# Whole-tensor loads in place of half loads in an attention and feed-forward kernel that plays a planned table

## The chip, the cores and the metric

The kernel runs on one core of a Trainium2 chip. The metric is the device time of one execution in microseconds (us). Everything below names the engines as the profile does: PE is TensorE's matmuls (PEld its weight loads), DVE is VectorE, ACT is ScalarE, POOL is GpSimd, SP is SyncE. SP computes nothing; it issues DMAs. An engine takes its instructions in the order in which they were put on its queue, and an instruction that waits holds up everything behind it on the same queue.

## The reference

Two stages follow each other. The first is a linear attention with a Hedgehog feature map over 8 batches, 8 heads, 576 positions and head size 64; the second is a feed-forward layer with a squared ReLU over the 4608 tokens.

```python
def phi(x):
    proj = np.einsum('bhsd,df->bhsf', x, w_phi)
    proj = proj - np.max(np.abs(proj), axis=-1, keepdims=True)
    return np.concatenate([np.exp(proj), np.exp(-proj)], axis=-1)
q_p, k_p = (phi(q), phi(k))
kv = np.einsum('bhsf,bhsd->bhfd', k_p, v)
z = np.sum(k_p, axis=2)
num = np.einsum('bhsf,bhfd->bhsd', q_p, kv)
den = np.einsum('bhsf,bhf->bhs', q_p, z)[..., None] + 1e-06
x = (num / den), tokens by 512
h = np.maximum(x @ w_in, 0.0)       # 512 x 2048
out = h * h @ w_out                 # 2048 x 512
```

## The kernel before

**Data.** All matmuls are in bfloat16. The loads convert from float32 on the way: GpSimd issues them (`load_x`, L341 to L354), and each q, k or v of a batch lands in a tile of 128 partitions (576 KB). Such a tile has four head pairs; batches 0 and 1 and the weights are loaded by a list of their own (`FIRSTS`, L359), and from batch 2 on `loads` (L378) issues two loads for each tensor, head pairs 0 to 1 and head pairs 2 to 3 (288 KB each). There are two buffers each for q, k and v.

**Attention of one batch.** k and q have to be transposed, so that head size lies on partitions. For batches 0 and 1 PE does it (L430) and DVE or ACT copies the result out. From batch 2 on, SP issues transposing DMAs (L419), five for k and five for q, each as soon as the part of the load that it reads has landed. kT has one buffer, qT has two. PE multiplies k with w_phi (L484), DVE takes the largest magnitude (L495) and subtracts it (L505), ACT takes the exponentials (L513; L529 in batches 0 and 1). POOL copies v into a tile with a column of ones (L466, L467) or, for the first parts of batches 0 and 1, scales v by an exponential of the maximum (L546). PE then forms kv, with the denominator as one more column (L579), in two halves of the heads, four products each; ACT or DVE copies it out (L594, L598). For each pair of 64-token groups PE projects q in two layouts (L625, L657), ACT takes the exponentials (L632), DVE and POOL prepare a scale (L664, L678, L687, L694), PE multiplies with kv (L725), and DVE finishes the quotient into a tile xo (L735, L742, L746). xo has three buffers. It is transposed into xT, by PE for batches 0 and 1 (L756, copied out at L761) and after that by a DMA that SP issues (L765).

**Feed-forward.** Nine chunks of 512 tokens. PE multiplies with w_in (L787), ACT takes the ReLU into hr (L792, three buffers), POOL squares it into h (L795, 30 buffers; DVE at L798 for chunks 7 and 8), PE multiplies with w_out (L818), DVE copies out (L835) and SP stores (L840, two DMAs for 128 tokens). The products of a chunk are mixed with the attention of later batches, so PE always has some of both to do. PSUM has eight banks, shared by all; the attention may hold seven.

**What sets the order.** The program is written as operations with engines, costs and dependences (`Plan.op`). A planner that is not part of the file has turned them into a table of numbers, `ORDER` (L93), one number for each operation in the order of their creation; a negative number stands for so many filling matmuls on PE (L384, warm-ups). `play` (L74) goes through the table, takes a buffer from a ring for an operation that is the first to use it, and emits the instructions. The waits that run on the chip are those that the data and the buffers need. The dependences and costs given to `op` served the planner alone: `load` (L293) makes each load depend on the issue of the one ahead, on a bound of 4096 descriptor rows, and, once 15 loads are queued, on the landing (`dma`, an operation without instructions) of the load two ahead. So in the order as planned two loads are outstanding.

Of the kernel before, what the change touches and what calls it, by code (L numbers as in the profile page):

```python
# [44 lines left out]
class Plan:  # L45
# [48 lines left out]
    7 9 11 6 13 15 17 19 10 1 2 8 4 5 -15 33 34 -3 50 54 51 16 -3 37 38 55 56 35 -1 72 39 52 36 57 59 53 73 74  # L94
    75 41 42 76 81 79 61 65 62 -6 94 40 -4 83 95 77 78 70 66 68 84 87 67 64 63 89 85 -2 43 44 18 -2 45 47 46 48
    -4 116 96 12 21 23 25 14 60 49 86 92 88 90 20 111 118 117 80 82 69 71 -1 100 102 58 91 115 114 97 93 27 29
    22 137 139 98 99 101 104 103 138 107 105 158 160 108 106 132 109 112 119 113 120 121 110 125 126 122 127
    159 133 136 135 134 140 128 153 154 161 157 179 123 129 124 141 142 146 147 130 131 155 156 181 143 144 148
    149 180 150 145 24 26 1465 1461 31 387 174 178 200 177 176 182 175 167 162 168 163 1462 169 164 1468 201
    170 165 171 202 1463 389 1466 1469 1470 1464 1467 166 183 214 215 151 216 188 184 189 152 195 198 199 197  # L100
    196 227 228 203 229 231 1471 185 190 218 186 1477 219 187 204 191 217 192 205 1472 1473 226 232 233 1478
    1474 1475 1476 1479 209 210 172 238 193 173 230 194 242 243 236 237 211 206 207 212 208 213 1480 239 244
    1481 247 1482 245 249 260 253 250 1494 1495 1490 256 257 246 240 1483 1486 241 234 1491 262 261 255 1487
    252 251 28 265 1508 30 220 222 267 221 223 224 225 266 235 1492 248 1489 1493 388 399 390 407 401 405 264
    258 254 259 1509 263 270 287 269 268 288 289 272 271 273 275 274 1510 1484 1496 391 393 1485 392 276 279
    278 303 306 305 277 308 309 310 304 280 281 290 307 32 1497 1501 1502 329 324 331 311 282 285 330 286 284
    283 1516 312 1504 1517 326 328 1505 327 325 332 394 1518 1506 1488 395 397 396 398 313 314 296 317 291 1507
    297 292 293 315 318 1511 316 298 299 300 294 400 1515 319 345 420 346 295 320 321 350 351 1519 301 347 322
    348 302 323 1498 1512 1522 349 1499 1513 1523 421 422 1520 1521 403 352 423 1526 1500 1514 402 371 373 372
    425 366 368 1527 353 1533 1525 354 1549 367 1534 369 1524 565 1535 567 1528 566 569 359 1532 333 427 426  # L110
    355 360 338 1529 1550 429 370 1530 424 428 1551 568 404 406 339 356 340 361 334 335 1539 362 341 363 357
    336 358 435 430 337 1536 374 1537 419 364 1546 365 342 437 436 1540 343 1541 344 438 439 571 1538 570 1531
    573 572 1555 1562 431 432 433 434 1547 1569 415 409 411 412 417 418 410 416 413 414 408 440 462 479 442 441
    443 1576 1577 1556 375 574 577 1548 589 579 583 1557 1573 464 376 380 1559 377 381 463 378 379 382 481 1558
    1542 480 483 482 1574 1560 1563 1564 444 484 383 384 486 485 575 0 1575 465 1561 487 446 447 453 445 506
    448 452 449 450 507 508 457 454 451 501 466 461 460 456 459 1552 1543 488 489 455 494 495 490 1553 458 1544
    576 591 593 509 1554 1579 504 1580 496 472 491 1566 385 492 497 473 498 493 467 474 468 475 476 1570 469
    470 471 503 502 745 1565 1581 747 1567 510 505 1571 386 1603 746 516 511 517 512 748 1503 499 477 580 603
    578 598 605 1585 513 518 514 519 515 520 521 604 1545 1589 1593 1597 1607 597 1572 1568 749 751 523 528 607
    526 524 1611 1615 600 599 601 527 529 530 1598 1616 581 582 478 500 522 1622 1623 1612 550 608 551 552 750  # L120
    752 602 525 1613 606 531 1624 753 1614 1600 1582 1630 609 610 1608 1601 1631 1583 553 755 1584 1632 585 586
    618 620 619 584 613 545 546 547 532 548 611 754 1609 612 1636 549 1637 1602 1610 1638 923 756 1640 1586
    1594 1595 554 1621 1587 1641 1642 1618 533 560 538 1625 590 592 587 1617 595 771 757 588 594 596 614 615
    1619 617 622 1596 925 1620 1588 621 534 539 555 684 1629 556 561 557 540 535 562 685 686 558 541 536 559
    542 1644 1633 563 564 537 1634 1604 1645 616 635 1605 924 662 663 664 636 639 637 638 758 630 631 632 624
    629 634 633 625 657 661 640 642 623 626 660 659 927 641 643 665 658 644 627 628 778 780 779 926 1639 1590
    650 1643 645 1591 666 687 929 928 1606 931 1592 646 651 679 728 730 1648 680 652 647 672 1647 653 729 731
    673 648 649 654 1651 769 1599 543 763 1578 761 775 759 667 674 1652 544 782 688 683 681 682 689 1626 1649
    1627 668 690 694 695 675 676 1675 696 691 669 670 692 671 693 697 698 1628 930 760 762 1679 706 701 783 708
    707 785 784 767 655 1683 705 703 704 702 781 1650 1646 1657 1661 1665 1687 709 710 786 723 726 724 764 788  # L130
    793 1688 1653 765 677 678 656 699 700 1669 794 1670 1676 1708 1694 727 787 1677 725 732 1695 1678 933 1712
    1662 1693 1697 770 776 772 773 774 1709 1710 1713 1663 777 795 789 790 791 792 766 768 820 815 798 822 1701
    821 738 739 800 799 1690 819 818 816 817 932 1103 1671 935 1635 1664 1696 1714 1691 1672 1720 1721 955 934
    953 797 1673 802 716 1666 717 740 741 711 733 718 712 734 1705 713 1706 719 714 735 1684 1658 801 736 742
    737 939 715 720 936 940 1674 1722 1692 1685 796 823 1659 1667 1668 1105 1660 1104 743 949 947 945 721 722
    951 937 1707 943 1689 812 806 842 843 844 804 805 803 808 807 809 810 811 813 837 838 814 840 841 839 956
    966 958 1654 1106 824 3 1655 1656 957 959 845 1107 1686 1109 1702 1680 1711 1715 830 1703 1681 846 968 831
    1719 825 826 832 847 852 848 853 833 967 1698 1704 1682 1699 1700 827 1723 849 854 1716 1717 1718 850 851
    828 855 856 834 1724 1729 970 1108 1733 859 860 908 829 938 1110 864 865 910 866 909 867 1111 1765 1769
    1773 863 862 861 868 969 881 886 887 961 884 885 744 835 857 941 836 858 1737 1741 963 888 1788 869 1744  # L140
    1742 874 1726 882 960 883 1745 1727 1113 889 1728 1738 962 964 875 870 876 1762 1739 1740 1763 911 1764
    1777 877 948 944 946 950 952 954 1020 976 1725 942 878 1021 978 1780 871 872 1022 873 1112 1789 890 1781
    965 1790 1746 1281 1730 1752 1747 1770 1753 1731 1114 1283 1782 1732 1778 977 980 971 903 906 907 972 973
    904 1771 912 1023 1754 1772 896 897 1784 1774 1751 1756 1775 905 974 1757 1758 918 891 892 1766 913 914 919
    1755 898 915 1785 1786 979 975 1767 1119 1117 1115 920 893 921 899 900 916 922 894 917 895 1743 879 1133
    1779 1127 1734 1759 1760 1116 1735 982 993 995 994 998 1000 999 1768 1001 984 981 983 996 1135 1736 1776
    997 1024 985 1002 986 988 990 1086 1087 1015 987 1016 1017 1018 989 1136 880 1783 1787 1791 991 992 1019
    1003 1025 1008 1748 1138 1137 1139 1749 1140 1026 1009 1030 1027 1801 1004 1031 1010 1032 1005 1006 1011
    1033 1028 1012 1007 1118 1795 1792 1793 1282 901 1131 1129 1120 1750 1805 1796 1034 1029 1088 1146 1147
    1042 1141 1142 1143 1044 1148 1013 1035 1121 1125 1123 1761 1809 1819 1823 1794 1827 902 1014 1036 1820  # L150
    1816 1810 1145 1821 1144 1043 1045 1817 1818 1811 1812 1822 1089 1284 1813 1814 1122 1150 1151 1064 1066
    1152 1059 1060 1061 1831 1832 1065 1153 1833 1842 1838 1824 1802 1062 1149 1063 1839 1843 1046 1825 1067
    1840 1285 1844 1826 1286 1124 1081 1085 1156 1037 1083 1038 1039 1041 1084 1068 1803 1040 1090 1157 1158
    1837 1841 1845 1860 1856 1861 1082 1857 1159 1804 1862 1287 1288 1047 1069 1070 1048 1834 1052 1071 1074
# [32 lines left out]
def kernel(  # L187
# [16 lines left out]
    NPR = H // 2  # L204
# [79 lines left out]
    queue, issues = [], []  # L284
# [77 lines left out]
    for n, what in enumerate(FIRSTS.split()):  # L362
        what, a = what.split(":")
        a, z = (int(x) for x in a.split("-"))
# [13 lines left out]
    def loads(b, dep):  # L378
        for name in "kvq":
            for a in range(0, NPR, 2):  # L380
                load_x(b, name, 32 * b - 120, dep, a, a + 2)
# [548 lines left out]
```

## Time and profile before

| | |
|---|---|
| median of 13 runs | 351.71 us |
| lowest, highest | 350.04, 357.43 us |
| the profiled execution's own time | 351.67 us |
| its span, first to last instruction | 349.9 us |
| granted TensorE clock | 1.00 |
| HBM read, written | 36.77 MB, 9.44 MB |
| loads of k, q, v in halves, issue to landing (median) | 5.4, 5.5, 6.0 us |
| transposing DMAs kT, qT, xT, issue to landing (median) | 5.3, 4.8, 3.1 us |

The profile is one execution taken by the hardware profiler. Its page gives busy time, 40 equal slices of 8.75 us with the busy share in tenths, the chain of work that ended last, groups of instructions and DMA issues. A row of a timeline has the start, the length, the engine, line, operation, tiles and shape, and in brackets the idle time just before it with what ended it. "SPq" is SP's queue; a wait of SPq is time in which nothing behind it on that queue could be issued.

### The profile page before, as it was taken

Reading aid. Unit: us, or ns where it says so; the run is one execution under the profiler, and the core shown is the slowest. Engines: PE = TensorE matmul, PEld = TensorE weight load, DVE = VectorE, ACT = ScalarE, POOL = GpSimd, SP = SyncE. Lnnn points to the kernel's source line nnn. Section 1 sums busy time; section 2 is a strip of 40 time slices with the busy share of each in tenths; the row PEclk is TensorE's granted clock in tenths of the full one; section 3 lists DMA queues with packets and bytes.
Section 4 is the critical chain, followed back from the end, with each engine's and each line's share of the span. In section 5 each row is a group of like instructions: output and inputs, shape, how many; then the busy total and the mean of one; then the engine's idle time right before and its main releaser. Section 6 shows DMA issues by size and latency. Waiting matters only on the chain.

```text
span 349.9 us, 10160 instructions
## 1 busy us (share of the span) xinstructions
PE 338.1 (97%) x4045; PEld 197.2 (56%) x4045; DVE 243.7 (70%) x553; ACT 242.2 (69%) x496; POOL 197.9 (57%) x305
## 2 busy tenths in 40 slices
PE   6899999989999999999999999998999999999995
PEld 4679777758645654565446544654546544544444
DVE  2999878985987898677766897767468446633531
ACT  4999997889488958895778649956795256703510
POOL 8957966848969672989397629945962020000000
PEclk9999999999999999999999999999999999999999
DMA  8999995998997993949986255784312323021134
GB/s 126 210 210 209 206 134 97 121 178 88 171 138 126 159 202 67 143 57 176 187 114 123 32 86 95 114 149 83 71 36 47 77 48 76 3 45 43 39 86 104
DMA packets 66527, 39.13 MB, mean 112 GB/s; under 512 B 46256, under 2 KB 60976, under 8 KB 66480
## 3 DMA queue, kind: packets, MB, share of 16 engines
q0 software_dynamic: 16144, 18.35, 36.4%
q1 hardware_dynamic: 50176, 20.00, 33.7%
q8 instruction: 31, 0.51, 0.6%
q10 hardware_dynamic: 160, 0.13, 0.2%
q14 instruction: 16, 0.13, 0.1%
HBM read 36.77 MB, written 9.44 MB: 132 GB/s over the span
## 4 chain that ended last, share of the span: by engine, by line
PE 78%; DMA 8%; DVE 5%; ACT 4%; SPq 3%; issue 1%; POOL 0%; DVEq 0%; POOLq 0%
PE one L787 31%; PE one L818 30%; PE one L725 5%; PE one L579 5%; DMA kT<-xk 2%; SPq L419 2%; PE one L625 2%; PE one L657 2%; DMA qT<-xq 2%; PE one L484 2%; DMA xk<-in_k_dram 2%; DVE mk L495 1%; DMA xT<-xo 1%; ACT hr L792 1%; ACT kph L513 1%
## 5 line engine op out<-in xcount | busy, mean ns | idle before, releaser
L795 POOL TENSOR_TENSOR h<-hr 128x512 bf16<-128x512 bf16 x112 | 114.4, 1039 | 52.8 <-ACT hr L792 49.1
L787 PE MATMUL one<-xT,win 128*128 128x512 bf16 (+2 forms) x768 | 138.5, 326 | 2.0 <-DVE xo L746 1.0
L818 PE MATMUL one<-wout,h 128*128 128x512 bf16 (+1 forms) x592 | 136.9, 374 | 0.0
L792 ACT ACTIVATE hr<-one 128x512 bf16<-128x512 f32 x144 | 84.8, 617 | 48.2 <-PE one L787 37.7
L632 ACT ACTIVATE qph<-one 128x512 bf16<-128x512 f32 (+1 forms) x160 | 81.4, 581 | 20.2 <-PE one L625 20.0
L787 PEld LDWEIGHTS <-win 128*128 128x128 bf16 x768 | 66.1, 98 | 50.8 <-issue 3.8
L818 PEld LDWEIGHTS <-h 128*128 128x128 bf16 x592 | 54.0, 98 | 56.2 <-issue 1.3
L513 ACT ACTIVATE kph<-ksh 128x1024 bf16<-128x1024 f32 (+1 forms) x66 | 62.2, 970 | 15.9 <-DVE ksh L505 15.8
L495 DVE TENSOR_REDUCE mk<-one 128x4 f32<-128x512 f32 (+1 forms) x80 | 49.6, 628 | 9.3 <-PE one L484 9.0
L687 POOL COPY mq<-m 64x4 f32<-64x4 f32 x108 | 19.9, 185 | 46.2 <-DVE m L678 42.4
L735 DVE TENSOR_TENSOR one<-one,em 128x260 f32<-128x260 f32 (+1 forms) x80 | 32.3, 431 | 19.3 <-PE one L725 14.5
L678 DVE TENSOR_REDUCE m<-one 128x4 f32<-128x512 f32 (+1 forms) x60 | 36.0, 631 | 13.8 <-PE one L657 10.2
L505 DVE TENSOR_TENSOR ksh<-one,mk 128x512 f32<-128x512 f32 (+1 forms) x66 | 41.4, 627 | 4.7 <-ACT kph L513 1.4
L725 PEld LDWEIGHTS <-qph 128*128 128x128 bf16 x640 | 30.9, 97 | 16.8 <-issue 0.7
L835 DVE COPY ot<-one 128x512 f32<-128x512 f32 x35 | 23.9, 686 | 19.1 <-PE one L818 18.9
L725 PE MATMUL one<-kv_sb,qph 128*128 128x65 bf16 x640 | 34.5, 194 | 0.7 <-DVE one L735 0.2
L746 DVE TENSOR_TENSOR xo<-one,rden 128x256 bf16<-128x256 f32 (+1 forms) x80 | 31.3, 416 | 3.5 <-DMA xT<-xo 2.6
L798 DVE TENSOR_TENSOR h<-hr 128x512 bf16<-128x512 bf16 x32 | 12.9, 420 | 13.8 <-ACT hr L792 13.5
L579 PE MATMUL one<-va,kph 64*128 64x65 bf16 x1152 | 21.9, 190 | 0.2 <-DVE ksh L505 0.2
L579 PEld LDWEIGHTS <-kph 64*128 64x128 bf16 x1152 | 20.3, 94 | 2.2 <-ACT hr L792 0.4
L742 DVE RECIPROCAL rden<-one 128x4 f32<-128x4 f32 (+1 forms) x80 | 11.7, 170 | 8.2 <-PE one L725 7.8
L657 PE MATMUL one<-wphi,qT 64*128 64x128 bf16 x296 | 15.4, 217 | 1.3 <-DMA qT<-xq 1.0
(46 smaller groups left out, 217.7 us busy)
## 6 DMA issues: line engine op xcount, KB each, us to landing
out_dram<-ot SPq DMA_DIRECT2D x70, 128.0 KB, 2.5
xv<-in_v_dram POOLq DMA_DIRECT2D x14, 288.0 KB, 6.0
xq<-in_q_dram POOLq DMA_DIRECT2D x14, 288.0 KB, 5.5
xk<-in_k_dram POOLq DMA_DIRECT2D x12, 288.0 KB, 5.4
win<-in_moe_w_in_dram POOLq DMA_DIRECT2D x2, 1024.0 KB, 14.7
wout<-in_moe_w_out_dram POOLq DMA_DIRECT2D x2, 1024.0 KB, 19.9
xk<-in_k_dram POOLq DMA_DIRECT2D x1, 576.0 KB, 18.8
xv<-in_v_dram POOLq DMA_DIRECT2D x1, 576.0 KB, 21.3
```

Source lines behind the costliest of these rows:

```text
L495: nc.vector.tensor_reduce(out=mk.t[:, e, ms], in_=wv(e), axis=AX.X, op=ALU.max, apply_absolute_value=True)
L505: nc.vector.tensor_tensor(out=ksh.t[:, e, : n // 2, :], in0=wv(e), in1=mk.t[:, e, ms].to_broadcast([P, n // 2, Fd]), op=ALU.subtract)
L513: nc.scalar.activation(out=t.t[:, :, : n // 2, :].rearrange("x e i f -> x e (i f)"), in_=ksh.t[:, :, : n // 2, :].rearrange("x e i f -> x ...
L579: nc.tensor.matmul(out=kvp(w, hi)[:, 2 * prl + s], lhsT=kph[g][s].t[r, i % 2, i // 2, :], rhs=va[s if g < nf else 0].t[r, u, : D + 1], sta ...
L632: nc.scalar.activation(out=t.t.rearrange("f (r b) hi p -> f b r hi p", b=2)[:, bk, :, :, lo:hi_], in_=w[bk].t[:, : nj * 256].rearrange("f ...
L678: d1 = [dve(kk, nj * 256, lambda w=w, m0=m0, nj=nj, bk=bk: nc.vector.tensor_reduce(out=m0.t[:, bk, : 2 * nj], in_=w[bk].t[:, : nj * 256].r ...
L725: nc.tensor.matmul(out=w.t[:, z * P : z * P + D + 1], lhsT=qg[s].t[:, h // 2, h % 2, :], rhs=kv[r][0].t[:, z % 2, z // 2, s, :], start=(s ...
L735: nc.vector.tensor_tensor(out=x, in0=x, in1=em.t[lo:hi_, hs].to_broadcast(list(x.shape)), op=ALU.mult)
L787: nc.tensor.matmul(out=w.t[:, y * n : (y + 1) * n], lhsT=win[:, kc, mc * P : (mc + 1) * P], rhs=xT.t[:, a:z, kc, :], start=(kc == 0), stop ...
L792: o = act(key - 4, TCH, lambda: nc.scalar.activation(out=r.t, in_=w.t, func=ACT.Relu), [p_], [w, r])
L795: o = pool(key - 4, 1050, lambda: nc.gpsimd.tensor_tensor(out=t.t, in0=r.t, in1=r.t, op=ALU.mult), [o], [r, t])
L818: nc.tensor.matmul(out=w.t[:, cols], lhsT=h2[c, mc, tt][0].t[:, h2[c, mc, tt][1] :][:, :P], rhs=wout[:, mc, cols], start=(mc == 0), stop=( ...
```

## The change

Three edits. `loads` issues one load for each tensor, all four head pairs at once, so 18 loads take the place of 36 in batches 2 to 7. In the planner's dependences a load, once 14 are queued, follows the landing of the one directly ahead. And the table was planned anew, with more slack for transfers. With 18 loads fewer the numbers of the table shift, so that almost every entry is another number.

```diff
@@ load
         i = pl.op("pool", 780, key, fn, list(deps) + (full if n > 4096 else []) + issues[-1:]
-                  + ([queue[-2][1]] if len(queue) >= 15 else []), bufs, lat=0)
+                  + ([queue[-1][1]] if len(queue) >= 14 else []), bufs, lat=0)
@@ loads
     def loads(b, dep):
         for name in "kvq":
-            for a in range(0, NPR, 2):
-                load_x(b, name, 32 * b - 120, dep, a, a + 2)
+            load_x(b, name, 32 * b - 120, dep)
@@ ORDER
-    7 9 11 6 13 15 17 19 10 1 2 8 4 5 -15 33 34 -3 50 54 51 16 -3 37 38 55 56 35 -1 72 39 52 36 57 59 53 73 74
+    7 9 6 11 13 15 17 1 2 19 8 -15 33 4 5 34 -3 50 54 55 10 51 53 52 -3 37 38 56 57 41 42 35 72 36 73 74 76 -1
...
```

Since every engine's order is the table's, it is moved on every engine. Numbering the operations in order of creation turns both tables into lists for each queue. What the prediction speaks of:

| queue | before | after |
|---|---|---|
| POOL, batch 0, behind the load of v of batch 1 | scaled v, plain copy of v, seven scaled v, loads of wout (first half), q of batch 1, wout (second half), k of batch 2 in two halves | scaled v, load of wout (first half), six scaled v, plain copy, scaled v, load of q of batch 1, two squarings, load of wout (second half), three squarings, load of k of batch 2 |
| POOL, batch 1, from the first squaring to the last scaled v | 8 squarings, plain copy, 6 scaled v | 10 squarings, plain copy, 6 scaled v, and the two loads named above |
| SP, first entries of batch 2 | four kT, the first output tile's stores, kT, five qT, kT of batch 3 | five kT, five qT, two pairs of stores, two kT of batch 3 |
| PE, filling matmuls | 41 | 37 |
| PE, last groups | products of w_out for chunk 8 | products of w_out for chunk 8 |

## The prediction, on record before the change was run

> **What bounds the kernel now.** I read the page first: the busy shares, the 40 slices, the chain; then TensorE's (PE's) timeline around every gap, then VectorE's, then the waits of SP, whose queue issues the transposing DMAs, and the loads by their line.
>
> ```profile
> span 349.9 us, 10160 instructions
> ...
> PE 338.1 (97%) x4045; PEld 197.2 (56%) x4045; DVE 243.7 (70%) x553; ACT 242.2 (69%) x496; POOL 197.9 (57%) x305
> ...
> PE   6899999989999999999999999998999999999995
> ...
> PEclk9999999999999999999999999999999999999999
> DMA  8999995998997993949986255784312323021134
> ...
> PE 78%; DMA 8%; DVE 5%; ACT 4%; SPq 3%; issue 1%; POOL 0%; DVEq 0%; POOLq 0%
> ```
>
> PE is busy for 97% of the span at full clock, so work beside PE is worth nothing. Only three things can move the time: PE's own work, the stretch before PE has work (the first 6), and gaps later. PE's timeline names the gaps (start, length, then in brackets the idle time before the row and what ended it):
>
> ```profile
> 74.14 0.28 PE L657 MATMUL one<-wphi,qT 64*128 64x128 bf16 x3 [0.70 <-DMA qT<-xq]
> 74.69 0.29 PE L657 MATMUL one<-wphi,qT 64*128 64x128 bf16 x4 [0.27 <-DMA qT<-xq]
> ...
> 86.62 0.39 PE L787 MATMUL one<-xT,win 128*128 128x256 bf16 x2 [0.45 <-issue]
> ...
> 104.62 0.51 PE L484 MATMUL one<-wphi,kT 64*128 64x128 bf16 x12 [0.43 <-DMA kT<-xk]
> ...
> 237.24 1.02 PE L787 MATMUL one<-xT,win 128*128 128x512 bf16 x4 [0.99 <-DVE xo L746]
> ```
>
> The last row waits for a bank that VectorE had not read out, and VectorE's timeline says why:
>
> ```profile
> 236.76 0.42 DVE L746 TENSOR_TENSOR xo<-one,rden 128x256 bf16<-128x256 f32 x1 [1.89 <-DMA xT<-xo]
> ```
>
> SP's waits show that four q transposes stood waiting for their loads (us in all, times, longest), and the line of the loads shows how long a load takes:
>
> ```profile
> SPq L419 <- DMA xq<-in_q_dram: 16.8, 4, 6.5
> ```
>
> ```profile
> DMA to landing us min/median/max: 3.6/5.6/24.1
> ```
>
> I took each PE group's step, start to next start, against the usual step of its kind: 0.86 for four 512-column matmuls, 0.22 to 0.23 for eight of L484 or L657, 0.29 for eighteen of L579, 0.12 for four of L725. After 24 us the excess is 4.6 in all. Three places make 3.0 of it, all late transposing DMAs: 1.37 at 73.2 (q of batch 2), 0.50 at 103.2 (k of batch 3), 1.16 at 235.2 (VectorE may not overwrite an xo buffer before its transpose has landed). The other 1.6 are small: 0.63 at 85.4 ("issue"), 0.25 at 204.8, 0.22 at 126.3, and less. Before 24 us PE waits on a chain that ScalarE (busy 10.00 of 10 in 10 to 20) and GpSimd (9.64) hold; GpSimd's and PE's timelines show where they meet:
>
> ```profile
> 11.14 7.33 POOL L546 TENSOR_TENSOR va<-xv,va 128x512 bf16<-128x512 bf16 x7 [0.21 <-ACT va L538]
> 18.41 0.95 POOL L373 DMA_DIRECT2D wout<-in_moe_w_out_dram  x1
> ```
>
> ```profile
> 18.52 0.75 PE L579 MATMUL one<-va,kph 64*128 64x65 bf16 x36
> ```
>
> After PE's last matmul, at 345.97, lie 3.9.
>
> The span is 349.9; this execution took 351.67, 1.77 more, and the median of 13 is 351.71. Half a percent, 1.75, is about what a measurement of this kernel tells from no change.
>
> **Part 1: 18 load instructions fewer.** Batches 2 to 7 issue 18 whole loads for 36 halves. GpSimd spends 0.75 on a half (its groups' mean) and 0.77 to 0.80 on the whole loads of batch 1, so about 13 are freed there. They hide behind PE: GpSimd is 57% busy and idles 49.1 waiting for hr. Gain: 0. If that cover went, GpSimd would only be freer. The new landing edge in `load` is one of the planner and the kernel plays a table, so no wait is added to any queue; only the places change.
>
> **Part 2: when a whole tensor lands.** No whole load on a quiet queue is in the trace; bounds come from halves issued back to back, by the landing that the trace has for each issue. From the first issue to the second landing: v of batch 2 6.05, q of batch 2 5.64, v of batch 4 9.1, q of batch 6 9.3. So a whole load takes 5.6 to 9.3; I take 7, the bulk of the cases being between. The 18 to 21 of batch 1 is a backlog (k, v, weights landed one after the other until 45.7) and sets no end. The first half's early landing is lost: 1.4 (q of batch 2, 4.23 against 5.64) to 4.3 (q of batch 6, 5.0 against 9.3), time in which some transposes could have begun.
>
> The Trainium skill, "DMA: Bandwidth & Descriptors", section "Anatomy of one DMA — SWDGE (gpsimd) path", gives 2.0 us plus bytes over 436 GB/s: an estimate of 3.4 for a whole tensor (0.59 MB) and 2.7 for a half. The halves took 5.6 in the median, so the trace does not agree. By that rule every load below would land some 3.6 earlier and the sum would be the same, because slack that is not used up is no time.
>
> **Part 3: the order on SP's queue, where the 3.0 lies.** The queue is in order: a transpose cannot be issued before the stores and xT transposes ahead of it have their data. I numbered both tables, added up PE's steps, and for each transpose took the PE work between the last thing its queue must wait for and its first use on PE. Five transposes cost 6.3 to issue (1.25 each) and land 2.4 (quiet) to 8.9 (loads beside them) later.
> - q of batch 2: before, a store that waits for the first output tile stands ahead, 17.5 of PE work in front of the use; one k and five q transposes then need 7.5 + 8.9, plus the store. It was 1.4 short. After, the five stand ahead of that store. What sets them is now the load. GpSimd reaches it near 52 (part 5's end at 47.4, a load of 0.8, three squarings, and slack), it lands by 58 to 61, issue ends by 67.5, landing by 70 to 76; PE asks at 70.4 + 6.3 = 76.7 (PE work ahead, plus 5.25 by which groups between 20 and 55 of PE work start later than their work in this trace, plus 1.0 for parts 4 and 5). No wait, margin 1 to 6.
> - k of batch 3: before, the last pieces had 7.8 and 11.6; after, 11.9 and 19.1.
> - xT, last piece before its chunk starts: before 5.8, 7.8, 8.5, 6.0, 5.2, 5.2, 5.2; after 8.5, 8.9, 8.6, 8.6, 7.8, 9.5, 9.5.
> - xo buffer: before, 8.0 was too little (the 1.16). After, that place has 18.2; the tightest up to PE work 290 is 7.9, at PE work 150.
> The 3.0 goes. What is late next is that 7.9 (0 to 1.2, by the row it resembles): I take 0.5. The small waits of 1.6 I leave.
>
> **Part 4: the start.** The issue of the first half of wout (0.95) moves ahead of GpSimd's scaled copies of v, and the plain copy (0.4 and a memset) goes from second to next to last. These copies run without a gap from 11.14 to 18.47, and the last kv product at 18.52 takes the last one at once. Work moved ahead of it costs up to 0.95; ScalarE then waits at its copy of kv (19.41 before). PE has small pieces to fill. Against it: four warm-up matmuls fewer, 0.9 of PE time that only fills waits. Bounds -0.4 to +1.0; I take +0.5. An earlier issue brings no earlier landing, as the queue is backed up until 45.7; the whole k of batch 2, issued near 35, still lands near 45.7.
>
> **Part 5: GpSimd in batch 1.** From the first squaring at 28.8 to the last scaled v took 15.0 before. After, up to the copy that kv's second product needs: 10 squarings of 1.01, five copies of 1.04, the plain copy 0.95, two loads 0.91 and 0.79: 17.95. The first squaring now takes the first hr and not the third, 1.0 sooner, and part 4 is 0.5 later: about 28.4. That ends at 46.35; PE asks at 40.3 + 5.25 + 0.5 = 46.05. Bounds 0 and 1.1 (start at 29.2, nothing won by the first hr); I take 0.5, about the middle.
>
> **Part 6: PE's changes of kind.** Between a 64-row and a 128-row group PE loses about 0.095 (0.957 for 0.861 after L818; 0.317 for 0.223 after L484). The table has 83 such changes before and 93 after: +0.95; the steps of all pairs, warm-ups aside, sum to only 0.5 more. I take 0.7. The last twenty PE groups end on the same two products and store, so the tail stays 3.9.
>
> **Sum.** -3.0 + 0.5 + 0.5 + 0.5 + 0.7 = -0.8; span 349.1, time **350.9**, 0.2% less: too little to tell.
>
> **The rivals.**
> *Faster:* the transfers' 3.0 goes and parts 4 and 5 cost nothing, with 0.5 in part 6: 349.9 - 3.0 + 0.5 + 1.77 = 349.2. For it: PE's slack for every transpose is wider after. Against it: GpSimd has no gap in 11 to 18, and 28 to 44 holds more before the same products.
> *Slower:* whole v and q of batch 2 go out 4 apart. If v, issued by 48.4, takes the upper 9.3 and q its 7 only after it, q lands at 64.7 and PE waits 64.7 + 6.3 + 8.9 - 76.7 = 3.2, on top of the sum: 354.1. It decides from a landing of 61.5 on. For it: q transposes landed 8.4 to 8.9 late with k of batch 3 beside them, and that load again falls near 62. Against it: both half pairs there took 6.05 and 5.64.
> *The change does not do what it says:* nothing at run time holds a load for the one ahead, whole loads crowd the transposes as long, and the 3.0 reappears elsewhere: 349.9 + 0.5 + 0.5 + 0.7 + 1.77 = 353.4. For it: DMA is above 0.9 busy through 130 us either way. Against it: part 3's counts.
>
> **How the numbers follow.** The sum 0.45 (350 to 352.5), faster 0.32, slower 0.13, gain lost 0.10. The gain-lost case lies on the edge and goes half to each side: faster 0.33, same 0.49, slower 0.18. The range, 348.6 to 353.9, leaves out the tail of the slower case and a luckier start.
>
> **What would show it.** Right: no PE gap put down to qT, kT or xo near 76, 110 and 237; the last kv product of batch 0 near 19.2 and ScalarE idle before its copy; a gap of up to 1 near 46 put down to va; whole loads landing in 6 to 9. Wrong: a q transpose of batch 2 landing after 77; GpSimd keeping PE from its first products past 24.5; new gaps of over 1 between VectorE and PE, which I counted only through the same slack and not instruction by instruction.

## The result and the profile after

The changed kernel is slower: 355.74 us in the median of 11 runs, against 353.22 of the kernel before (48 runs). The ratio is 1.0114, 95% interval 1.0083 to 1.0145, about 4 us; the two medians lie only 2.5 apart because the kernel before has slow executions among its runs (up to 358.80), and the ratio compares fast ones alone. The prediction was 350.9, 0.2% faster, with a range that ended at 353.9. The profiled execution took 356.58; its span is 354.8, 4.9 more than the span of before.

The page of the changed kernel (its line numbers are 3 lower than before's in the body of the kernel), and under it the chain of work that ended last, by engine:

```profile
span 354.8 us, 10124 instructions
...
PE 341.3 (96%) x4041; PEld 198.3 (56%) x4041; DVE 243.2 (69%) x553; ACT 243.9 (69%) x496; POOL 185.8 (52%) x287
...
PE   6889999999989999999999899999999999999995
...
PEclk9899999999999999999999999999999999999999
DMA  7999949694898999667974794555510340321413
...
PE 78%; DMA 9%; DVE 7%; ACT 3%; issue 2%; POOL 0%; DVEq 0%; ACTq 0%; POOLq 0%
```

GpSimd is freed as expected (197.9 busy before, 185.8 after), and it moves nothing. The chain has more DMA and DVE than before and no SPq. The waits of the changed kernel (us in all, times, longest) name what is new, the transposes of xo into xT:

```profile
PE one L784 <- DMA xT<-xo: 2.0, 3, 1.2
DVE xo L743 <- DMA xT<-xo: 1.9, 1, 1.9
PE one L576 <- issue: 1.3, 1, 1.3
PE one L427 <- DMA xk<-in_k_dram: 2.3, 1, 2.3
```

Before, PE had no wait of the first kind. The old waits for q of batch 2, k of batch 3 and the xo buffer at 235 have gone. The last row is at 9: one load of the first batch came in late in this execution and PE's clock was granted at 0.93 up to 24 us. Both kernels have executions with and without that (the changed kernel's second profile has it too, and so has the third experiment's, which has the order of before), so below the start is read from profiles that are free of it. The chain, in order of time (start, us, what), shows how long the critical transposes took:

```profile
95.89 7.70 DMA xT<-xo
133.22 6.03 DMA xT<-xo
158.44 5.91 DMA xT<-xo
166.90 6.70 DMA xT<-xo
```

And the issues of transfers in the stretch from 94.5 to 96 (tile, queue, number, KB, median us to landing) show what went out beside the first of them:

```profile
xk<-in_k_dram POOLq DMA_DIRECT2D x1, 576.0 KB, 7.9
xT<-xo SPq DMA_TRANSPOSE x1, 7.7
```

The whole load of k of batch 4 was issued at 95.35, 0.5 us ahead of the last transpose that chunk 2 needed (95.89). On its own such a transpose lands in 2.4; before, this one landed in 3.1. In all four rows of the chain a load had gone out 0.5 to 1.8 us ahead of the transpose (the others at 131.69, 156.63 and 165.92), and the transpose landed 0.4 to 0.9 after that load: the loads at 103.22, 138.51, 163.48 and 172.93, the transposes at 103.59, 139.24, 164.35 and 173.60. PE's timeline has the price:

```profile
103.64 3.63 PE L784 MATMUL one<-xT,win 128*128 128x512 bf16 x16 [1.20 <-DMA xT<-xo]
```

I took the steps of all PE groups against the usual step of their kind, as for the prediction. What they lose by stretch (us), for the two profiles of the changed kernel (the second is the first experiment's) and for those that matter below:

| stretch | before | after | after, second | after, no loads | four loads later | that, head of before |
|---|---|---|---|---|---|---|
| 0 to 24 | 4.1 | 6.7 | 6.4 | 5.9 | 5.9 | 3.9 |
| 24 to 60 | 0.2 | 1.3 | 1.0 | 1.2 | 0.7 | 0.9 |
| 60 to 130 | 2.7 | 1.9 | 2.1 | 0.6 | 0.6 | 0.6 |
| 130 to 200 | -0.1 | 3.8 | 4.5 | 1.2 | 1.3 | 1.0 |
| 200 to 260 | 1.4 | 0.2 | 0.2 | 0.2 | 0.2 | 0.2 |
| 260 to the end | 0.1 | -0.2 | -0.2 | -0.2 | -0.2 | -0.2 |
| sum of usual steps | 335.3 | 334.9 | 334.9 | 334.9 | 334.9 | 336.0 |

(The last column also has one group of products moved, the eighth experiment below.) The difference of the first two columns, 5.3 lost and 0.4 won on the usual steps, is the 4.9 between the spans. The usual steps count the filling products, of which the changed order has four fewer: 0.9 by the prediction's figure. So without them the changed order's usual steps are 0.5 more; and if they only filled waits, as the prediction has it, 0.9 of what the first stretch loses more is no time of its own (the tenth experiment bears this out).

### The profile page after: what moved, and what is told of

Its sections match the earlier page's. It is cut to its first block, busy times and chain, and to the rows that moved or that the text cites. A ratio compares the mean times of both kernels' runs of the same rounds, so it can differ in the third digit from the quotient of the medians.

```text
span 354.8 us, 10124 instructions
## 1 busy us (share of the span) xinstructions
PE 341.3 (96%) x4041; PEld 198.3 (56%) x4041; DVE 243.2 (69%) x553; ACT 243.9 (69%) x496; POOL 185.8 (52%) x287
## 4 chain that ended last, share of the span: by engine, by line
PE 78%; DMA 9%; DVE 7%; ACT 3%; issue 2%; POOL 0%; DVEq 0%; ACTq 0%; POOLq 0%
PE one L784 33%; PE one L815 29%; DMA xT<-xo 7%; PE one L722 5%; PE one L576 4%; DMA xk<-in_k_dram 2%; PE one L622 2%; PE one L481 2%; PE one L654 2%; DVE mk L492 2%; DVE xo L743 1%; DVE m L675 1%; ACT kph L510 1%; ACT qph L629 1%; DVE one L732 1%
## 5 line engine op out<-in xcount | busy, mean ns | idle before, releaser
L789 ACT ACTIVATE hr<-one 128x512 bf16<-128x512 f32 x144 | 83.4, 603 | 49.6 <-PE one L784 37.5
L722 PE MATMUL one<-kv_sb,qph 128*128 128x65 bf16 x640 | 36.0, 194 | 0.9 <-DVE one L732 0.5
L739 DVE RECIPROCAL rden<-one 128x4 f32<-128x4 f32 (+1 forms) x80 | 12.3, 171 | 10.8 <-PE one L722 10.1
L526 ACT ACTIVATE kph<-one 128x512 bf16<-128x512 f32 x28 | 15.6, 622 | 1.0 <-PE one L481 0.7
```

Source lines behind the costliest of these rows:

```text
L722: nc.tensor.matmul(out=w.t[:, z * P : z * P + D + 1], lhsT=qg[s].t[:, h // 2, h % 2, :], rhs=kv[r][0].t[:, z % 2, z // 2, s, :], start=(s ...
L789: o = act(key - 4, TCH, lambda: nc.scalar.activation(out=r.t, in_=w.t, func=ACT.Relu), [p_], [w, r])
```

## The experiments

**Theories.** Theory 1, place: a load that is issued just ahead of a chunk's last xT transposes makes them land in 6 to 8 us, and PE or VectorE waits. Theory 2, in three forms: the size of a load does it (2a); the new order at the start costs it (2b); the new order of PE does it elsewhere, by changes of kind or by instruction fetch. The expectations call the tile xo, the attention's quotient, "exp"; the transposes meant are those of xo into xT. Line numbers in the experiments on the changed kernel are one higher than in the changed kernel (four in the sixth), and in the third and the eleventh one higher than in the kernel before.

### 1 to 3: the changed kernel again, and both kernels without the later loads

For the second and third run, which leave out the loads of batches 2 to 7:

```diff
-        parts.append((a * NJ, load(key, 295 * (z - a), 128 * (z - a), fn, [dep], [buf])))
+        parts.append((a * NJ, load(key, 295 * (z - a), 128 * (z - a), fn if b < 2 else None, [dep], [buf])))
```

> The changed kernel itself, on one chip beside the three that follow. Theory 1 (crowding): a whole load of 0.59 MB that is issued 0 to 5 us ahead of a chunk's last transposes of exp makes those land in 6 to 8 us instead of 2.4 to 4.3, and TensorE and the exp buffers wait 3.2 to 3.5 us for them. Theory 2 (the order): the new order of all engines' work costs the 3 us by itself (changes of kind on TensorE, the start, instruction fetch), whatever the loads do. Both expect 1.007 to 1.014 times the kernel before. What this profile tells: the waits at 101 (1.4 us), 139 (0.4), 165 (1.1) and 172 (0.7) should be there again with landings of 5.9 to 7.7 behind them (theory 1; by theory 2 they may come and go); the 2.3 us wait for the second half of batch 1's k near 9 should be gone if it was a matter of that one execution, and so should the 1.3 us without a named cause near 196.

> The changed kernel with the loads of batches 2 to 7 left out (their buffers keep what batches 0 and 1 brought; all other work is done on it). Theory 1: the transposes of exp land in 2.4 to 3.0 throughout, the four waits (3.5 us) go, and the time is 3 to 4 us below the changed kernel's, at 350 to 351.5 where the kernel before stands at 352 to 353. Theory 2: within 1 us of the changed kernel's time.

> The kernel before with the loads of batches 2 to 7 left out in the same way. Theory 1: its three transfer waits (1.37 at 73, 0.50 at 103, 1.16 at 235) go or shrink to under half, so 1.5 to 3 us below the kernel before, and within 0.8 us of the changed kernel without its loads: the two orders are worth the same once no load stands in the way. Theory 2: it is 3 us or more below the changed kernel without its loads.

Measured, on one chip: the changed kernel 356.59 (1.0121 times the kernel before, 1.0065 to 1.0177); without loads 352.10 (0.9984, 0.9947 to 1.0022); the kernel before without loads 349.18 (0.9911, 0.9874 to 0.9948). The waits of the changed kernel's second profile:

```profile
PE one L785 <- DMA xT<-xo: 3.2, 2, 1.8
DVE xo L744 <- DMA xT<-xo: 2.3, 1, 2.3
PE one L577 <- issue: 0.7, 1, 0.7
```

Sorted by PE's steps: 1.5 at 101, 1.9 at 138, 1.5 at 166, and again about 1 in the run of small products near 196. The wait at 172 did not come back, that at 138 was larger. So the places stay roughly, the sizes vary from execution to execution.

Without loads all waits for xT go. The tile xT's own account in that run (all its transposes, issue to landing) against the changed kernel's:

```profile
DMA to landing us min/median/max: 2.4/2.4/4.5
```

```profile
DMA to landing us min/median/max: 2.4/3.1/7.7
```

The loads cost the changed order 4.5 us (356.6 to 352.1), more than the 3 to 4 of theory 1. But theory 2 has a share, where I had expected one theory or the other: without any later load the changed order is still 2.9 above the kernel before (352.1 to 349.2), where theory 1 had the two within 0.8. The table by stretch says where: 0 to 24, 24 to 60 and the run near 191.

One old wait was put down wrongly. Of before's three, those at 73 and 103 go without the loads, but the one at 235 stays, here in PE's timeline of before without loads:

```profile
235.84 1.02 PE L788 MATMUL one<-xT,win 128*128 128x512 bf16 x4 [1.19 <-DVE xo L747]
```

Its transposes landed late because they were issued late. It is a matter of the order, not of the loads.

### 4: four loads later

In the changed table, k of batch 4, v of batch 5, k and v of batch 6 are moved in GpSimd's queue (the number in brackets is the load; the table's numbers are those of the changed kernel). Between the two profiles they move by 3.2, 8.3, 10.1 and 15.9 us. The loads' order among themselves does not quite stay, as the expectation says it does: v of batch 5 and v of batch 6 now go out behind q of the same batch.

```diff
-1562 589 525 [733] 1536
+1545 1532 547 [733] 734 585
...
-717 773 698 [907] 1602
+1630 774 909 [907] 908 1631
...
-790 826 825 [1079] 806
+870 931 871 [1079] 1080 1683
...
-1642 869 870 [1081] 931
+1732 1696 893 [1081] 1082 1720
```

> The changed kernel with four of its eighteen whole loads (k of batch 4, v of batch 5, k of batch 6, v of batch 6) issued later in GpSimd's queue, behind the work that stands beside the last transposes of exp of the chunk at hand (about 4, 5, 15 and 21 us later); size, number and the order of the loads among themselves stay. Theory 1: the transposes at 101, 139, 159 and 172 land in under 4.5 and their waits go: 2.5 to 3.5 us below the changed kernel. What could give part of it back: k of batch 4 and 6 and v come in later and their own transposes may become late (up to 1 us). Theory 2: within 0.8 us of the changed kernel.

Measured: 352.13 us, 1.0023 times the kernel before (0.9986 to 1.0061), 4.5 below the changed kernel on the same chip. That is more than the 2.5 to 3.5 expected. The stretch from 60 to 200 loses 1.9 in place of 5.7 and 6.6; with no loads at all it loses 1.8. The tile xT of this run:

```profile
DMA to landing us min/median/max: 2.4/2.5/4.9
```

With the same eighteen loads, of the same size, the transposes land nearly as if there were no loads, and the time is that of no loads (352.10). Four places made the transfers' cost.

The size of that cost is less sure than its place. Both profiles of the changed kernel have the late first load and a granted clock of 0.995. In the executions with 0.998 or more the median of the changed kernel is 354.41 (nine, with those of the result) and of this one 351.74 (seven): 2.7 apart and not 4.5.

### 5 and 6: size without place, place without size

The fifth kernel is the kernel before, with a whole load at the place of each first half:

```diff
-            for a in range(0, NPR, 2):
-                load_x(b, name, 32 * b - 120, dep, a, a + 2)
+            load_x(b, name, 32 * b - 120, dep)
```

The sixth is the changed table with each whole load split into two halves one behind the other.

```diff
-            load_x(b, name, 32 * b - 120, dep)
+            for a in range(0, NPR, 2):
+                load_x(b, name, 32 * b - 120, dep, a, a + 2)
```

> The kernel before, its order of work untouched, with the whole-tensor load of every tensor from batch 2 on at the place of its first half (18 issues in place of 36). If the size of a load were what delays the transposes of exp (theory 2a), this kernel gains waits of 2 us and more: 1.006 times the kernel before or above. If it is the place alone (theory 1), the waits stay where they were: within 0.8 us of the kernel before, and any new wait stands where a load happens to be issued under 5 us ahead of a chunk's last transposes.

> The changed kernel, its order untouched, with each of its eighteen whole loads issued as two halves back to back at the same place. Theory 1 (place): the same bytes stand beside the same transposes, so the waits at 101, 139, 165 and 172 stay and the time is within 1 us of the changed kernel (1.009 to 1.015 times the kernel before). Theory 2a (size): the transposes land in under 5 again, the waits go, and it is 3 us or more below the changed kernel.

Measured: the fifth 353.31 (1.002, 0.9975 to 1.0066), the sixth 356.06 (1.0102, 1.0032 to 1.0172). Halves at the changed kernel's places are as slow as whole loads there: the critical transposes landed behind the second half (second halves at 102.94, 137.47 and 163.07, transposes at 103.00, 137.97 and 165.40). The waits of the sixth:

```profile
DVE xo L747 <- DMA xT<-xo: 3.9, 1, 3.9
PE one L788 <- DMA xT<-xo: 1.2, 1, 1.2
```

That speaks against size. The fifth settles less. Its old waits at 73 and 103 went or shrank, but new ones came at 68 (0.9), 118 (1.8) and 172 (1.4). The first is a kT transpose that landed at 68.81, 0.2 after a whole load issued beside it; the last ended 0.1 after the landing, at 174.14, of an xT transpose that had gone out at 169.90, 0.4 ahead of a whole load. The one at 118 stands behind ScalarE's work with no DMA in its chain, and its cause stays open. The interval of the fifth does not quite exclude the 1.006 that the size theory asked for.

### 7 and 10: the start

Both kernels take the order of all engines from the kernel before up to a time, and the changed order with the four loads later for the rest. The seventh cuts at 58 us, the tenth at 26 (183 of the table's entries). The tenth also has the moved products of the eighth. In words:

```diff
-ORDER = changed table
+ORDER = before's table up to its cut, then what is left of the changed table, in its order
```

> The changed kernel with its four loads issued later, and with the kernel before's order of all engines' work up to 58 us (what follows is in the changed kernel's order). In the changed kernel's order TensorE loses 5.9 us over its usual steps up to 24 us and 0.7 to 1.2 us from 24 to 60; in the kernel before's 4.1 to 4.9 and 0.2. If the start is a cost of the order (theory 2b), this kernel is 1.2 to 2.8 us below the kernel with four loads later (352.1 on the same count); if it is only another start of the loads from one execution to the next, it is within 0.6 us of it.

> The kernel with four loads later and one product earlier, with the kernel before's order of all engines up to 26 us, where the two tables have nearly the same work behind them (5 entries differ), so that the seam costs next to nothing. If the order of the start costs the 1.5 us by which TensorE's first 24 us lose more in the changed order (6.1 in the mean of six profiles against 4.5 in three), the time is 1.0 to 1.8 below 350.9, at 349.1 to 349.9. If those 1.5 are only the fortune of single executions, it is within 0.4 of 350.9.

The seventh missed: 355.56 (1.0122, 1.0086 to 1.0159). The profile shows why it tells nothing of the start. PE lost 4.6 between 60 and 67, just behind the cut, where the two orders did not fit (rows of PE's timeline):

```profile
62.17 0.21 PE L655 MATMUL one<-wphi,qT 64*128 64x128 bf16 x1 [1.17 <-DVE ksh L503]
63.49 0.38 PE L655 MATMUL one<-wphi,qT 64*128 64x128 bf16 x7 [1.11 <-DVE ksh L503]
```

From 60 to 68 PE's clock was granted at 0.79, so the two idle gaps cost about as much again in slow products; I saw no such clock where PE stayed busy.

The tenth, with a cut where the two tables have nearly the same work behind them: 350.05 (0.9898, 0.985 to 0.9946), all six runs between 349.71 and 350.31. That is 0.9 below the eighth (350.94, on another chip), just short of the 1.0 to 1.8 that the order of the start was to cost, and more than the 0.4 of mere fortune. Up to 24 us PE loses 3.9, close to before's 4.1, and not 5.9 as in the fourth, but before's head also has the four filling products, 0.9 by their usual steps. What is left shows directly in PE's timeline: with before's head the first products with w_out begin at 38.59, in the fourth experiment, whose order is the same from the cut to there, at 39.43. The order of the start costs about 0.9 us. The 0.9898 flatters: the fastest execution of the kernel before beside it took 351.46, and on the other two chips 349.32 and 349.05.

### 8: one group of products moved

At 188 to 192 PE has a run of some 150 small products. Four products with w_out (entry 1747), which stood behind it, are moved into its middle:

```diff
-964 969 965 [1747] 1738
+862 960 963 [1747] 1019
```

> The changed kernel with its four loads issued later, and with one group of TensorE's work (the four 512-wide products of out that stood behind a run of some 150 products of 64 to 128 columns at 188 to 192) moved into the middle of that run; nothing else is moved. The changed order waits 0.9 to 1.5 us in that run in all four executions profiled so far, for nothing that the profile names, about 2 us after a 16 KB fetch of instructions was begun. If TensorE runs through its instructions faster there than they are fetched, four wide products (0.87 us) in the middle give the fetch time and 0.7 to 1.1 us of the wait go: 351.1 to 351.5 where the kernel with four loads later stands at 352.1. If the wait has another cause, it stays: within 0.3 us.

Measured: 350.94 (0.9975, 0.9939 to 1.001), a little below the 351.1 to 351.5 expected; but the interval overlaps that of the fourth, which ran on another chip beside other executions of before. The place itself is clear. PE's timeline of the changed kernel, and then of this one:

```profile
194.37 1.55 PE L576 MATMUL one<-va,kph 64*128 64x65 bf16 x87
197.23 0.22 PE L576 MATMUL one<-va,kph 64*128 64x65 bf16 x3 [1.31 <-issue]
```

```profile
190.30 0.73 PE L577 MATMUL one<-va,kph 64*128 64x65 bf16 x36
190.96 1.04 PE L816 MATMUL one<-wout,h 128*128 128x512 bf16 x4
191.93 1.11 PE L577 MATMUL one<-va,kph 64*128 64x65 bf16 x54
```

The wait stood in every profile of that order (0.9 to 2.0 by PE's steps) and is gone. In this execution 0.5 of it came up a little later, at 194.3 to 195. It fits with a fetch of instructions: in the fourth experiment's profile a 16 KB transfer of the instruction queue began at 189.53 and took 1.16, and PE stood from 191.0 to 192.0. That the fetch is the cause is argued from this and from the cure, not shown by itself.

### 9: the issue of wout

The load of the first half of wout (entry 27) goes back behind the last scaled copy of v, in the kernel of the eighth.

```diff
-23 25 58 [27] 14 80 60
+107 105 93 [27] 98 119
```

> The changed kernel with four loads later and the one product earlier, and with the issue of the first half of wout put back behind the last scaled copy of v of batch 0 in GpSimd's queue, where the kernel before has it. The last scaled v ended at 20.0 in the changed order and at 18.5 before. If GpSimd's place of that issue is the cost of the start (part 4 of the prediction), the last scaled v ends 0.8 to 0.95 sooner, TensorE's first 24 us lose 0.5 to 0.9 less, and the time is 0.5 to 0.9 below that of the kernel with one product earlier (350.9). If the start's cost is TensorE's and ScalarE's own new order, it is within 0.3 us of it.

Measured: 351.59 (0.9948, 0.9913 to 0.9982), no more than the eighth gave within their intervals. Between executions in which the first scaled v began at the same 9.7, the last one ended at 18.63 here and at 19.21 in the fourth experiment, 0.6 sooner where 0.8 to 0.95 were expected, and PE's first products with w_out began at 39.11 and 39.43. With before's head they began at 38.59. So this issue is worth some 0.3 of the 0.8 between them; the rest lies in the order of the other work at the start, and which engine's is not separated.

### 11: loads put beside transposes in the kernel before

```diff
-866 909 867 [1111] 1765 ... 883 1745 1727 [1113] 889
+1704 1682 [1111] [1113] 1699
...
-1825 1067 1840 [1285] 1844 ... 1159 1804 1862 [1287] 1288
+1120 1750 [1285] [1287] 1805
```

> The kernel before with two pairs of half loads moved, nothing else: q of batch 6 from 168.6 to about 164, just ahead of the last two transposes of exp for chunk 4 (issued 165.4 and 166.7, landed 169.6 and 170.1, used 171.1), and v of batch 7 from 215.8 and 221.0 to about 199.5, just ahead of the last two for chunk 5 (issued 200.4 and 201.9, landed 202.8 and 205.9, used 206.0). Theory 1 (place): these transposes land in 5.5 to 8, and TensorE waits 0.5 to 2.5 at 171 and 1.5 to 4 at 206: 2 to 5 us above the kernel before (1.006 to 1.014). If a load beside a transpose is harmless in this order, within 0.8 us of the kernel before.

Measured: 360.28 us, 1.0196 times the kernel before (1.0138 to 1.0255), more than the 1.014 that I gave as the upper end. The chain that ended last, from 198 to 214:

```profile
203.31 7.31 DMA xT<-xo
```

and PE's timeline:

```profile
174.05 1.02 PE L788 MATMUL one<-xT,win 128*128 128x512 bf16 x4 [1.71 <-DVE ot L836]
...
211.22 4.19 PE L788 MATMUL one<-xT,win 128*128 128x512 bf16 x12 [2.42 <-DMA xT<-xo]
```

The first row names VectorE, but the chunk's last transpose landed at 173.96, 0.1 before it. Before, the two transposes of the second place landed in 2.4 and 4.0. By PE's steps 1.9 was lost at 171, 2.8 at 207 and 1.7 more in the five microseconds behind that, where PE's clock was granted at 0.57 (212 to 216). PE also waited 1.2 longer than before for kT at 101, where no load was moved; so not all of this execution's excess is theirs. Two pairs of half loads, issued 4 and 14 to 18 us earlier, and nothing else changed, make the order of before 2% slower. Place is enough.

## Why the prediction was wrong

Step by step, as the prediction had them.

- **Part 1, fewer issues, gain 0.** Right: GpSimd has 12.1 us less to do and idles longer for hr.
- **Part 2, a whole load lands in 7, at 5.6 to 9.3.** Right: sixteen or more of the eighteen in either profile took 5.8 to 9.3; k of batch 2, behind the weights, took 9.7 and 10.4, and q of batch 2 once 9.35.
- **Part 3, "The 3.0 goes", plus 0.5 for what is late next. This is the step that failed.** The three old waits did go. In their place stood 3.5 us of new ones in the first profile (1.4 at 101, 0.4 at 139, 1.1 at 165, 0.7 at 172) and 4.9 in the second. The 0.5 for the xo buffer "at PE work 150" is the one at 165, and it cost 1.1 and 1.5. The other three are the chunks to which I gave a slack of 8.5, 8.9 and 8.6 and then no cost. My own figures forbade that: 1.25 for each of two issues and a landing of up to 8.9 "with loads beside them" make 11.4. I compared the slack with the landings of before, 2.4 to 4.3 for the last two transposes of those chunks, and did not ask what stood beside them after. That needed GpSimd's queue beside SP's, and I had numbered each table queue by queue. The 1.16 at 235 was also not a late landing beside loads (third experiment).
- **Part 4, the start, 0.5.** Low, but within its bounds of -0.4 to 1.0: about 0.9 (tenth experiment). The reason was only in part right: the issue that I costed makes some 0.3 (ninth), and the rest of the start's order I did not price. That it stayed within the bounds is luck.
- **Part 5, 0.5 near 46.** The stretch from 24 to 60 loses 0.5 to 1.1 more than before in the four columns with the changed start, about 0.9 in the mean, in pieces of 0.2; no wait for va stands near 46.
- **Part 6, 0.7 for changes of kind.** By the count of usual steps it is the 0.5 that the prediction names beside it: they sum to 0.4 less with four filling products (0.9) fewer. No run tests it alone.
- **Not in the sum.** The wait in the run of small products, 0.9 to 1.5 in the changed kernel; the one of before at 85, 0.6, went.

With what was measured in place of the terms: -3.0 - 0.6 + 4.2 + 0.9 + 0.9 + 1.2 + 0.5 = +4.1 (4.2 and 1.2 being the means of the two profiles), against the 4.0 of the ratio. The close agreement is in part chance: both profiles are of executions with the late first load, while the start is taken from others. Without the 4.2 the same sum is -0.1, and that is the kernel with four loads later, level with the kernel before (1.0023).

**The rivals.** The third, that whole loads crowd the transposes and the 3.0 reappears, came nearest, at 353.4 by its price and a 0.10 chance; but it is the place that crowds them and not that the loads are whole (sixth experiment). The second came half true: q of batch 2 landed at 62.84, past the 61.5 from which I had PE wait, but no wait came, since its transposes landed within 2.4 to 7.1 and not the 8.9 that I had put behind it.

## What to carry to other kernels

When loads move in an in-order queue, take every transfer on whose landing the end depends and ask what will be in flight beside it after the change; a slack is to be set against the landing in that company, not against the one in the old trace. A planner that gives a transposing DMA one fixed latency cannot see this; moving four loads by 3 to 16 us was worth 2.7 to 4.5 us here. And where a table is planned anew, test its pieces by joining the old head to the new rest, at a time at which both have done the same work: the joined kernel of the tenth experiment beats both, as its six runs, up to 350.31, lie under each run of the kernel before beside them (351.46 and more).

## What the runs showed of the hardware

- A transposing DMA of one 128-token tile of xo lands in 2.4 us on quiet queues. Those that ended waits in the two profiles of the changed kernel had gone out within 2 us behind a load of 0.59 MB, took 5.9 to 7.8 and landed 0.4 to 1.0 after the load. With the load in two halves, one behind the other, the one at 95 still took 7.7. What makes them land behind the load is not shown.
- Two idle gaps of 1.2 and 1.1 us on PE, close together, went with a granted clock of 0.79 over the 8 us around them, and one of 2.4 with 0.57 from 212 to 216 (eleventh experiment); the gap of 2.3 at 9 us went with 0.93 up to 24. Gaps of 1.8 at 140 (first experiment) and 2.1 at 166 (sixth) went with a full clock, so the length of a gap alone does not tell.
- A run of about 90 products of 64 rows in 1.55 us was followed by a wait of about 1 us that the profile puts down to no semaphore; four wide products in its middle took it away.
